# Block 0's first four shifts summed first, mean times power on GpSimd, and two weight slabs placed behind block 0's transposes

## The chip, the core and the metric

The kernel runs on one core of a Trainium2 chip. A core has five engines with an instruction queue each: TensorE (PE, matmuls), VectorE (DVE), ScalarE (ACT), GpSimd (POOL) and SyncE (SP, which here issues only transfers). Each works through its queue in order and waits at an instruction until the semaphores it needs have been raised. Transfers run on 16 DMA engines that all queues share. The metric is the device time of one execution in microseconds; lower is better.

## The reference

Four layers follow each other on one sequence of 2048 tokens with 1024 features: attention (A), feed-forward (B), and both again with the same weights. Each reads a normalised copy of the residual stream `x` and adds its result to it.

```
def _A_ref(x, wqkv, wo):
    H = 32; Dh = D // H;  W, dil = 8, 2
    q, k, v = split((x @ wqkv), heads)
    idx = pos[:, None] - dil * arange(W)[None, :]        # 8 keys: the own one and 7 earlier, 2 apart
    logits = einsum("bhsd,bhswd->bhsw", q, kg) * Dh**-0.5 # masked where idx < 0
    attn = softmax(logits)
    return einsum("bhsw,bhswd->bhsd", attn, vg) @ wo
def _B_ref(x, W_gate, W_up, W_down):
    return ((relu(x @ W_gate)) * (x @ W_up)) @ W_down     # F = 3584
x = x + _A_ref(_layernorm(x), A_wqkv, A_wo)
x = x + _B_ref(_layernorm(x), B_W_gate, B_W_up, B_W_down)
x = x + _A_ref(_layernorm(x), A_wqkv, A_wo)
x = x + _B_ref(_layernorm(x), B_W_gate, B_W_up, B_W_down)
```

The attention is a sliding window of 8 dilated positions, so its logits and its weighted sum are elementwise products and sums on VectorE; only the projections and the feed-forward are matmuls. All inputs are bf16.

## The kernel before

**Blocks and layers.** The tokens are cut into four blocks of 512 (four tiles of 128). For each layer L and block b there are steps: `plan_ln` (layer norm), `plan_proj` (q, k, v), `plan_attn` (logits, softmax, weighted sum), `plan_wo` (output projection and residual add), `plan_gu` (gate and up) and `plan_down`. L counts 0 (attention), 1 (feed-forward), 2 (attention), 3 (feed-forward).

**The order is written out by a planner.** Nothing is reordered later. Every step is put down with a planned time (`Plan.at`), and `Plan.run` (lines 116 to 120) sorts the steps by it and emits them; this fixes the order in every engine's queue. TensorE's planned time advances 0.216 us per matmul (`on_pe`). VectorE's steps come in two kinds. `plan.chain` is a long list, worked off in order, of the attention's products and sums. `plan.on_dve` steps (residual adds, gate multiplies, statistics) have a due time and go in between as soon as it is reached (`_place_dve`, lines 85 to 106). A load of a weight slab is placed when one of the five ring slots comes free, and not before the slab's `start` (`_place_slabs`, lines 108 to 114; `start` is -10.0 if nothing is given). The planner's times order the work; they are not the chip's.

**Weights.** Slabs are 1 MB (1024 rows by 512 columns) and go through the ring of five. `plan_gu` takes one gate and one up slab for four groups of 128 columns each.

**Layer norm.** `plan_ln` (lines 209 to 303) works on pairs of tiles. It gets sum and sum of squares from ScalarE (`stats`, lines 235 and 236), or statistics from VectorE (`bn`). `small_a` (239 to 258) computes mean and variance on VectorE and 1/sqrt on GpSimd as a power (line 257, or 247). `small_b` (260 to 263) multiplies -mean by it on VectorE. `norm` (265 to 270) applies both on ScalarE. `turn` (272 to 278) transposes a pair with a transfer issued by SyncE; the pair becomes half of `xnT`, the operand of the matmuls that follow.

**Block 0 of the first attention** has its logits computed in another layout (`first_logits`, lines 457 to 528). As each of the eight 128-row chunks of q and k leaves TensorE, VectorE multiplies it for all eight shifts (`mul`, line 488) and adds the product to two accumulators, shifts 0 to 3 (h=0) and 4 to 7 (h=1) (`add`, line 499). Each accumulator is then stored to DRAM (line 505), loaded again with heads on the partitions (line 510) and folded (`fold`, lines 524 and 525). Both accumulators end with the last chunk, so both stores, and both loads, follow each other closely. The softmax and the weighted sum (`pv_mul`, `pv_add`) come next, then the loads of the result (`load_o`, line 623) and the output projection `wo(0, 0)`. That is planned inside block 3's projection, behind its group ("q", 1, 1), by the table `wo_hook` (line 791).

**What follows wo(0, 0) on the engines.** TensorE goes on with the rest of block 3's q, with k and with v, and then starts `plan_gu(1, 0)`, which reads `xnT` of layer 1, block 0. On the other engines the residual adds (line 690), the norm and the two transposes of that block run meanwhile. On SyncE, between those transposes, stand loads of slabs for `plan_gu(1, 0)`, because two ring slots come free when block 3's k is done.

**Pools.** The tag "T" of the pool `tpose` has four buffers of 8 KB per partition, shared by `xnT`, the accumulators `lacc` and the attention outputs `oT`. The tags "q" and "k" of `hm_pool` have one buffer each.

Of the kernel before, what the change touches and what calls it, by code (L numbers as in the profile page):

```python
# [123 lines left out]
def kernel(  # L124
# [84 lines left out]
    def plan_ln(L, b, lag=0.5, on_vector=False, norm_at=0.0):  # L209
        hold = {}  # L210
        clock = [0.0]

        def begin():
            hold["xn"] = ln_pool.tile([P, TPB, D], BF16, tag="xn_all", name="xn_all")
            hold["T"] = tpose.tile([P, TPB, KC, P], BF16, tag="T", name=f"xnT_{L}_{b}")

        def bn(t):
            def f():
                if t == 0:
                    begin()  # L220
                if t % 2 == 0:
                    hold[("bn", t // 2)] = stat_pool.tile([P, 2, 2, 6], F32, tag="bst2", name="bst2")
                for h in range(2):
                    nc.vector.bn_stats(hold[("bn", t // 2)][:, t % 2, h, :], x_tiles[b * TPB + t][:, 512 * h:512 * h + 512])
            return f

        def stats(t):
            def f():
                if t == 0:
                    begin()  # L230
                if t % 2 == 0:
                    hold[("st", t // 2)] = stat_pool.tile([P, 2, 2], F32, tag="st", name=f"st_{L}_{b}")
                st, xt = hold[("st", t // 2)], x_tiles[b * TPB + t]
                junk = hold["xn"][:, t, :]
                nc.scalar.activation(junk, xt[:], ACT.Identity, accum_out=st[:, 0, t % 2:t % 2 + 1])
                nc.scalar.activation(junk, xt[:], ACT.Square, accum_out=st[:, 1, t % 2:t % 2 + 1])
            return f

        def small_a(p):
            rstd = stat_pool.tile([P, 2], F32, tag="rstd", name="rstd")  # L240
            vpe = stat_pool.tile([P, 2], F32, tag="vpe", name="vpe")
            if on_vector:
                mv = stat_pool.tile([P, 2, 2], F32, tag="mv2", name="mv2")
                for i in range(2):
# [5 lines left out]
            st = hold[("st", p)]  # L250
            mean = stat_pool.tile([P, 2], F32, tag="mean", name="mean")
            nc.vector.tensor_scalar(mean[:], st[:, 0, :], 1.0 / D, None, op0=ALU.mult)
            nvar = stat_pool.tile([P, 2], F32, tag="nvar", name="nvar")
            nc.vector.tensor_tensor(nvar[:], st[:, 0, :], mean[:], op=ALU.mult)
            nc.vector.tensor_tensor(nvar[:], nvar[:], st[:, 1, :], op=ALU.subtract)
            nc.vector.tensor_scalar(vpe[:], nvar[:], -1.0 / D, EPS, op0=ALU.mult, op1=ALU.add)
            nc.gpsimd.tensor_tensor(rstd[:], vpe[:], neg_half[:, 0:2], op=ALU.pow)
            hold[("mean", p)], hold[("rstd", p)] = mean[:], rstd

        def small_b(p):  # L260
            nb = stat_pool.tile([P, 2], F32, tag="nb", name="nb")
            nc.vector.scalar_tensor_tensor(nb[:], hold[("mean", p)], -1.0, hold[("rstd", p)][:], op0=ALU.mult, op1=ALU.mult)
            hold[("nb", p)] = nb

        def norm(t):
            def f():
                i, rstd, nb = t % 2, hold[("rstd", t // 2)], hold[("nb", t // 2)]
                nc.scalar.activation(hold["xn"][:, t, :], x_tiles[b * TPB + t][:], ACT.Identity,
                                     scale=rstd[:, i:i + 1], bias=nb[:, i:i + 1])
            return f  # L270

        def turn(t):
            def f():
                nc.sync.dma_start_transpose(hold["T"][:, t - 1:t + 1].rearrange("p t k n -> p (t k) n"),
                                            hold["xn"][:, t - 1:t + 1].rearrange("p t d -> p (t d)"))
                if t == TPB - 1:
                    xnT[(L, b)] = hold["T"]
            return f

        def row_done(t):  # L280
            def f(now):
                e = max(clock[0], now + 0.3)
                if on_vector:
                    plan.on_dve(e, 1.4, bn(t))
                    clock[0] = e + 1.4
                else:
                    plan.at(e, stats(t))
                    clock[0] = e + 2.6
                if t % 2 == 1:
                    plan.on_dve(clock[0], 0.7, lambda: small_a(t // 2), lambda n: after_a(n, t))  # L290
# [12 lines left out]
        return [row_done(t) for t in range(TPB)]  # L303
# [151 lines left out]


    def first_logits(st, tm):
        hold = {}

        def begin():  # L460
            hold["q"] = hm_pool.tile([P, KC, BLK], BF16, tag="q", name="q_fm")
# [3 lines left out]
        def evict(nm, c, acc, t):  # L465
            def f():
                if nm == "q":
                    nc.scalar.copy(hold["q"][:, c, :], acc()[:])
                    return
                kt = hold["k"]  # L470
                nc.scalar.copy(kt[:, c, HALO:HALO + BLK], acc()[:])
                nc.gpsimd.dma_start(_dram(k_d[1], c * ROW, [[D // P * ROW, P], [1, HALO]]),
                                    kt[:, c, BLK:BLK + HALO])
            if nm == "q" and c == 0:
                plan.at(t - 1.0, begin)
            plan.at(t, f)
# [8 lines left out]
        def mul(c):  # L485
            def f():
                pr = at_pool.tile([P, W, BLK], BF16, tag="pr", name=f"prod_{c}", bufs=2)
                nc.vector.tensor_tensor(pr[:], _ap(hold["q"], c * BLK, [[0, W], [1, BLK]]),
                                        _ap(hold["k"], c * ROW + HALO, [[-DIL, W], [1, BLK]]), op=ALU.mult)
                hold[("pr", c)] = pr  # L490
            return f

        def add(c, h):
            def f():
                if c == 1:
                    hold[("acc", h)] = tpose.tile([P, TPB, W // 2, P], F32, tag="T", name=f"lacc{h}")
                acc = hold[("acc", h)][:].rearrange("p q w t -> p w q t")
                first, more = (hold[("pr", i)][:, 4 * h:4 * h + 4].rearrange("p w (q t) -> p w q t", q=TPB) for i in (0, c))
                nc.vector.tensor_tensor(acc, first if c == 1 else acc, more, op=ALU.add)  # L499
            return f  # L500

        def turn(h):
# [15 lines left out]

        def fold(h):
# [181 lines left out]
    def plan_gu(L, b):  # L701
# [199 lines left out]
```

## Time and profile before

| | us |
|---|---|
| median of 3 runs | 1627.84 (1627.81 to 1628.78) |
| profiled execution | 1628.73 |
| its span, first to last instruction | 1627.0 |
| TensorE busy | 1610.5 (99%) |
| VectorE busy | 1059.3 (65%) |
| ScalarE busy | 441.7 (27%) |
| GpSimd busy | 104.2 (6%) |
| granted TensorE clock, mean | 0.998 |

Times in the views count from the span's start. A line of the order of time gives start, duration, engine, line of the kernel, operation, what it writes and reads, and in brackets how long the engine stood idle before it and what ended that. SPq and ACTq are issues of transfers; their durations are those of the issue. When a transfer has landed is told by a separate line, "DMA to landing". Waits name the engine and line that waited, what ended the wait, the sum, the count and the longest. The releaser is inferred from semaphores and can be the wrong one where an instruction waits for several.

### The profile page before, as it was taken

To read this page: it belongs to the slowest core of one execution; us is meant where nothing else is said; L and a number is where in the kernel's file an instruction comes from. 1 tells how busy PE (TensorE), PEld (TensorE's weight loads), DVE (VectorE), ACT (ScalarE), POOL (GpSimd) and SP (SyncE) were. 2 spreads that over 40 slices of the span, in tenths; PEclk is the share of its full clock that TensorE was granted. 3 is DMA by queue.
4 is the path that set the end of the run, shared out by engine and by line. 5 is a ranking of instruction groups with operands and counts; after the bars stand their busy time and mean duration, and the time that the engine had idled before them with its cause. 6 is when DMAs were issued, how large, how long until landed. Compare 5 with 4: busy or idle time off the path is not lost.

```text
span 1627.0 us, 19118 instructions
## 1 busy us (share of the span) xinstructions
PE 1610.5 (99%) x7577; PEld 745.2 (46%) x7626; DVE 1059.3 (65%) x1286; ACT 441.7 (27%) x701; POOL 104.2 (6%) x169
## 2 busy tenths in 40 slices
PE   9999899999999999999999999999999999999999
PEld 6444344444444444444444444444444444444444
DVE  6979889999999359870699716996989212211211
ACT  4642511304230341312413151133021301221110
POOL 2221000001000100011000110000000000000000
PEclk9999999999999999999999999999999999999999
DMA  8997767978956989568886699599846755665452
GB/s 249 219 245 162 201 153 203 217 198 203 240 161 193 258 192 225 172 210 222 199 214 188 197 235 215 159 281 243 217 152 196 196 168 162 174 177 160 156 163 69
DMA packets 445162, 319.01 MB, mean 196 GB/s; under 512 B 195696, under 2 KB 437776, under 8 KB 444816
## 3 DMA queue, kind: packets, MB, share of 16 engines
q1 hardware_dynamic: 415904, 285.59, 66.7%
q10 hardware_dynamic: 24368, 23.40, 4.9%
q0 software_dynamic: 4800, 8.80, 1.7%
q8 instruction: 59, 0.97, 0.3%
q14 instruction: 31, 0.25, 0.1%
HBM read 263.86 MB, written 38.15 MB: 186 GB/s over the span
## 4 chain that ended last, share of the span: by engine, by line
PE 89%; DVE 6%; DMA 2%; issue 1%; ACT 1%; POOL 0%; SPq 0%; ACTq 0%; DVEq 0%; POOLq 0%
PE acc_g L713 24%; PE acc_u L713 24%; PE dacc L759 24%; PE acc_wo L683 6%; PE acc_k L397 4%; PE acc_q L397 4%; PE acc_v L397 4%; DVE pvt L604 1%; DVE lacc L499 1%; DVE l L563 1%; DVE pvt L612 1%; DVE pr L553 1%; DMA v_d<-stage_v 0%; DMA lhm<-l_d 0%; DMA k_d<-stage_k 0%
## 5 line engine op out<-in xcount | busy, mean ns | idle before, releaser
L713 PEld LDWEIGHTS <-ring 128*128 128x128 bf16 x3584 | 350.9, 98 | 432.3 <-DMA v_d<-stage_v 7.7
L713 PE MATMUL acc_g<-xnT,ring 128*128 128x512 bf16 x1792 | 425.0, 380 | 7.2 <-DMA v_d<-stage_v 7.2
L713 PE MATMUL acc_u<-xnT,ring 128*128 128x512 bf16 x1792 | 423.9, 380 | 0.0
L759 PE MATMUL dacc<-ring,hT 128*128 128x512 bf16 (+1 forms) x1787 | 386.4, 376 | 1.7
L728 DVE TENSOR_TENSOR hT<-acc_u,r 128x512 bf16<-128x512 f32 x224 | 154.4, 689 | 329.1 <-PE acc_u L713 322.6
L720 ACT ACTIVATE r<-acc_g 128x512 bf16<-128x512 f32 x224 | 133.5, 596 | 713.1 <-PE acc_g L713 713.1
L759 PEld LDWEIGHTS <-hT 128*128 128x128 bf16 x1820 | 178.0, 98 | 209.1
L397 PEld LDWEIGHTS <-ring 128*128 128x128 bf16 x1152 | 115.5, 100 | 133.2 <-DMA ring<-in_A_wqkv_dram 0.3
L604 DVE TENSOR_TENSOR pvt<-a,vhm 128x4096 bf16<-128x4096 bf16 x64 | 146.2, 2284 | 0.2
L563 DVE TENSOR_TENSOR l<-l,pr 128x1024 f32<-128x1024 f32 x112 | 136.8, 1221 | 2.2
L553 DVE TENSOR_TENSOR pr<-qhm,khm 128x4096 bf16<-128x4096 bf16 x56 | 127.9, 2284 | 14.7 <-DMA khm<-k_d 14.7
L397 PE MATMUL acc_k<-xnT,ring 128*128 128x512 bf16 x512 | 113.2, 379 | 0.0
L683 PE MATMUL acc_wo<-ring,oT 128*128 128x512 bf16 x496 | 111.0, 379 | 0.8
L767 DVE TENSOR_TENSOR xb<-dacc,xb 128x512 bf16<-128x512 f32 (+1 forms) x49 | 32.6, 679 | 120.9 <-PE dacc L759 120.7
L397 PE MATMUL acc_v<-xnT,ring 128*128 128x512 bf16 x384 | 84.2, 379 | 0.0
L612 DVE TENSOR_TENSOR pvt<-pvt 128x2048 bf16<-128x2048 bf16 x64 | 78.1, 1221 | 1.3
L683 PEld LDWEIGHTS <-oT 128*128 128x128 bf16 x512 | 50.0, 98 | 60.5
L615 POOL DMA_DIRECT2D o_d<-ohm x64 | 35.2, 550 | 647.6 <-DVE ohm L614 634.5
L406 ACT CAST stage_q<-acc_q 128x512 bf16<-128x512 f32 x56 | 32.3, 582 | 153.6 <-PE acc_q L397 147.5
L563 DVE TENSOR_TENSOR l<-pr 128x1024 f32<-128x1024 bf16 x56 | 68.3, 1219 | 0.6
L570 DVE TENSOR_TENSOR l<-l 128x512 f32<-128x512 f32 x112 | 62.3, 556 | 2.9
L397 PEld LDWEIGHTS <-wqv 128*128 128x128 bf16 x480 | 44.8, 104 | 40.7 <-issue 1.4
(84 smaller groups left out, 807.8 us busy)
## 6 DMA issues: line engine op xcount, KB each, us to landing
ring<-in_B_W_gate_dram SPq DMA_DIRECT2D x56, 1024.0 KB, 7.3
ring<-in_B_W_up_dram SPq DMA_DIRECT2D x56, 1024.0 KB, 5.5
ring<-in_B_W_down_dram SPq DMA_DIRECT2D x48, 1024.0 KB, 6.0
ring<-in_A_wqkv_dram SPq DMA_DIRECT2D x26, 1024.0 KB, 5.4
ring<-in_A_wo_dram SPq DMA_DIRECT2D x16, 1024.0 KB, 7.1
vhm<-v_d SPq DMA_DIRECT2D x32, 284.0 KB, 7.1
v_d<-stage_v ACTq DMA_DIRECT2D x32, 256.0 KB, 7.0
o_d<-ohm POOLq DMA_DIRECT2D x64, 128.0 KB, 4.0
```

The costliest lines, as they stand in the source:

```text
L397: nc.tensor.matmul(acc[:, t0 * P:t1 * P], lhsT=lhsT, rhs=xnT[(L, b)][:, t0:t1, kc, :], start=(kc == 0), stop=(kc == KC - 1))
L553: nc.vector.tensor_tensor(pr[:], st["q"][:], _ap(st["k"], HALO - DIL * w, [[HALO + P, DH], [1, P]]), op=ALU.mult)
L563: nc.vector.tensor_tensor(l[:], pr[:, 0:8] if i == 0 else l[:], pr[:, 8 * i + 8:8 * i + 16], op=ALU.add)
L570: nc.vector.tensor_tensor(l[:, 0:n], l[:, 0:n], l[:, n:2 * n], op=ALU.add)
L604: nc.vector.tensor_tensor(tt[:], a_bc, v_sh, op=ALU.mult)
L612: nc.vector.tensor_tensor(tt[:, 0:4], tt[:, 0:4], tt[:, 4:8], op=ALU.add)
L615: nc.gpsimd.dma_start(_dram(o_d[b], g * DG * P, [[DH * P, P], [1, DG * P]]), o[:].rearrange("p d t -> p (d t)"))
L683: nc.tensor.matmul(acc[:], lhsT=st["oT"][:, c, t, :], rhs=ws[half]["t"][:, c, :], start=(c == 0), stop=(c == KC - 1))
L713: nc.tensor.matmul(acc[:], lhsT=w["t"][:, kc, (j % 4) * P:(j % 4 + 1) * P], rhs=xnT[(L, b)][:, :, kc, :], start=(kc == 0), stop=(kc == KC ...
L720: nc.scalar.activation(r[:], hold.pop(("g", j))[:], ACT.Relu)
L728: nc.vector.tensor_tensor(st["hT"][:, j, :], hold.pop(("u", j))[:], hold.pop(("r", j))[:], op=ALU.mult)
L759: nc.tensor.matmul(accs[(t, c0)][:], lhsT=st["hT"][:, j, t * P:(t + 1) * P], rhs=w["t"][:, jl, c0 - half * SLAB:c0 - half * SLAB + n], sta ...
```

## The change

There are five edits.

- In `first_logits`, chunks 0 to 3 stay as they are. Chunks 4 to 7 are multiplied in halves: first the four shifts of h=0 for all four chunks, each with its addition, then the four shifts of h=1. The h=0 accumulator's store and load are thus planned about 14 us ahead of those of h=1, and its fold stands directly behind the last addition. The h=0 load now goes to a buffer of the tag "T", the h=1 load to the tag "q". The planned time from an accumulator's end to its load's landing is 9.5 instead of 11.0.
- In `plan_ln`, -mean is kept in `neg` (VectorE), and GpSimd multiplies it by the power. `small_b` and its VectorE step are gone; `after` plans the normalise 1.8 behind `small_a`.
- In `plan_gu`, all slabs but the first pair of layer 1, block 0 may not be placed ahead of planned time 174.0. This touches the second pair only, since the others come later anyhow.
- `wo(0, 0)` is hooked behind the group ("q", 1, 0), eight matmuls earlier.
- The sign of the variance's parts is turned to suit `neg`; the number of instructions stays.

```
@@ plan_ln
         def small_a(p):
+            neg = stat_pool.tile([P, 2], F32, tag="neg", name="neg")
+            nb = stat_pool.tile([P, 2], F32, tag="nb", name="nb")
             if on_vector:
...
-                nc.gpsimd.tensor_tensor(rstd[:], vpe[:], neg_half[:, 0:2], op=ALU.pow)
-                hold[("mean", p)], hold[("rstd", p)] = mv[:, :, 0], rstd
-                return
+                nc.vector.tensor_scalar(neg[:], mv[:, :, 0], -1.0, None, op0=ALU.mult)
+            else:
+                st = hold[("st", p)]
+                nc.vector.tensor_scalar(neg[:], st[:, 0, :], -1.0 / D, None, op0=ALU.mult)
+                var = stat_pool.tile([P, 2], F32, tag="var", name="var")
+                nc.vector.tensor_tensor(var[:], st[:, 0, :], neg[:], op=ALU.mult)
+                nc.vector.tensor_tensor(var[:], var[:], st[:, 1, :], op=ALU.add)
+                nc.vector.tensor_scalar(vpe[:], var[:], 1.0 / D, EPS, op0=ALU.mult, op1=ALU.add)
             nc.gpsimd.tensor_tensor(rstd[:], vpe[:], neg_half[:, 0:2], op=ALU.pow)
-        def small_b(p):
-            nc.vector.scalar_tensor_tensor(nb[:], hold[("mean", p)], -1.0, hold[("rstd", p)][:], op0=ALU.mult, op1=ALU.mult)
+            nc.gpsimd.tensor_tensor(nb[:], neg[:], rstd[:], op=ALU.mult)
...
-        def after_a(now, t):
-            plan.on_dve(now + 1.3, 0.2, lambda: small_b(t // 2), lambda n: after_b(n, t))
-        def after_b(now, t):
-            e = max(clock[0], now + 0.2, norm_at)
+        def after(now, t):
+            e = max(clock[0], now + 1.8, norm_at)
@@ first_logits
             if nm == "k":
-                plan.chain.append((lambda: t + 0.7, 2.3, mul(c), None))
-                for h in range(2 if c else 0):
-                    plan.chain.append((lambda: 0.0, 2.3, add(c, h), turn(h) if c == KC - 1 else None))
+                ready[c] = t + 0.7
+                for h in range(2 if c == KC - 1 else 1):
+                    for c in range(KC // 2, KC) if h else (c,):
+                        whole = c < KC // 2
+                        plan.chain.append((lambda c=c: ready[c], 2.3 if whole else 1.2, mul(c, None if whole else h), None))
+                        for i in range(2 if whole else 1) if c else ():
+                            plan.chain.append((now, 2.3, add(c, i if whole else h), turn(h) if c == KC - 1 else None))
...
             def load():
-                hold[("l", h)] = hm_pool.tile([P, FG, W // 2, P], F32, tag="qk"[h], name=f"lhm{h}")
+                pool, tag = ((tpose, "T"), (hm_pool, "q"))[h]
+                hold[("l", h)] = pool.tile([P, FG, W // 2, P], F32, tag=tag, name=f"lhm{h}")
...
-                tm[("l_in", h)] = now + 11.0
+                tm[("l_in", h)] = now + 9.5
@@ plan_gu
-                sl = {"g": slab(wg_v[:, :, c0:c0 + SLAB], f"wg_{L}_{b}_{j // 4}"),
-                      "u": slab(wu_v[:, :, c0:c0 + SLAB], f"wu_{L}_{b}_{j // 4}")}
+                hold_back = 174.0 if (L, b) == (1, 0) and j else -10.0
+                sl = {"g": slab(wg_v[:, :, c0:c0 + SLAB], f"wg_{L}_{b}_{j // 4}", hold_back),
+                      "u": slab(wu_v[:, :, c0:c0 + SLAB], f"wu_{L}_{b}_{j // 4}", hold_back)}
@@
-    wo_hook = {("q", 1, 1): lambda: wo(0, 0)}
+    wo_hook = {("q", 1, 0): lambda: wo(0, 0)}
```

More of the change, by code (lines that the diff above doesn't have):

```diff
@@ L246, in small_a @@
                 nc.vector.tensor_scalar(vpe[:], mv[:, :, 1], EPS, None, op0=ALU.add)
-                nc.gpsimd.tensor_tensor(rstd[:], vpe[:], neg_half[:, 0:2], op=ALU.pow)
-                hold[("mean", p)], hold[("rstd", p)] = mv[:, :, 0], rstd
-                return
[L250 to L258, printed above, removed]
-        def small_b(p):
-            nb = stat_pool.tile([P, 2], F32, tag="nb", name="nb")
-            nc.vector.scalar_tensor_tensor(nb[:], hold[("mean", p)], -1.0, hold[("rstd", p)][:], op0=ALU.mult, op1=ALU.mult)
-            hold[("nb", p)] = nb
+                nc.vector.tensor_scalar(neg[:], mv[:, :, 0], -1.0, None, op0=ALU.mult)
[6 more added lines that the diff above has]
+                nc.vector.tensor_scalar(vpe[:], var[:], 1.0 / D, EPS, op0=ALU.mult, op1=ALU.add)
+            nc.gpsimd.tensor_tensor(rstd[:], vpe[:], neg_half[:, 0:2], op=ALU.pow)
+            nc.gpsimd.tensor_tensor(nb[:], neg[:], rstd[:], op=ALU.mult)
+            hold[("rstd", p)], hold[("nb", p)] = rstd, nb
         def norm(t):
@@ L289, in f @@
                 if t % 2 == 1:
-                    plan.on_dve(clock[0], 0.7, lambda: small_a(t // 2), lambda n: after_a(n, t))
+                    plan.on_dve(clock[0], 0.7, lambda: small_a(t // 2), lambda n: after(n, t))
             return f
-        def after_a(now, t):
-            plan.on_dve(now + 1.3, 0.2, lambda: small_b(t // 2), lambda n: after_b(n, t))
-        def after_b(now, t):
-            e = max(clock[0], now + 0.2, norm_at)
+        def after(now, t):
+            e = max(clock[0], now + 1.8, norm_at)
             plan.at(e, norm(t - 1))
@@ L457, in first_logits @@
     def first_logits(st, tm):
-        hold = {}
+        hold, ready = {}, {}
+        now = lambda: 0.0
         def begin():
@@ L483, in evict, with mul @@
                                        (lambda now: tm.__setitem__("logits", now)) if h else None))
-        def mul(c):
+        def mul(c, h):
             def f():
[L487 to L490, printed above, removed]
+                w, n = (0, W) if h is None else (W // 2 * h, W // 2)
+                pr = at_pool.tile([P, n, BLK], BF16, tag="pr", name=f"prod_{c}", bufs=2)
+                nc.vector.tensor_tensor(pr[:], _ap(hold["q"], c * BLK, [[0, n], [1, BLK]]),
+                                        _ap(hold["k"], c * ROW + HALO - DIL * w, [[-DIL, n], [1, BLK]]), op=ALU.mult)
+                for i in range(2) if h is None else (h,):
+                    hold[("pr", c, i)] = pr[:, W // 2 * i - w:W // 2 * (i + 1) - w].rearrange("p w (q t) -> p w q t", q=TPB)
             return f
@@ L497, in f @@
                 acc = hold[("acc", h)][:].rearrange("p q w t -> p w q t")
-                first, more = (hold[("pr", i)][:, 4 * h:4 * h + 4].rearrange("p w (q t) -> p w q t", q=TPB) for i in (0, c))
-                nc.vector.tensor_tensor(acc, first if c == 1 else acc, more, op=ALU.add)
+                nc.vector.tensor_tensor(acc, hold[("pr", 0, h)] if c == 1 else acc, hold[("pr", c, h)], op=ALU.add)
             return f
```

## The prediction

> **What bounds the kernel now.** I read the page first, then TensorE's waits, then the order of time around the one long wait, and last the engines ahead of it. The page:
>
> ```profile
> span 1627.0 us, 19118 instructions
> ...
> PE 1610.5 (99%) x7577; PEld 745.2 (46%) x7626; DVE 1059.3 (65%) x1286; ACT 441.7 (27%) x701; POOL 104.2 (6%) x169
> ```
>
> TensorE is busy for 1610.5 of 1627.0 us. The change takes no matmul away, so it can only win back idle or slowed matmul time. TensorE's own waits, all of them:
>
> ```profile
> PE acc_g L713 <- DMA v_d<-stage_v: 7.2, 1, 7.2
> PE warm L317 <- POOL neg_half L183: 1.4, 1, 1.4
> PE acc_v L397 <- DVE xnT L359: 0.9, 1, 0.9
> PE acc_v L397 <- ACT xnT L359: 0.5, 2, 0.2
> PE tp L356 <- DVE xn_all L351: 0.4, 1, 0.4
> ```
>
> One wait matters: 7.2 us ahead of the first gate matmul. The name of its releaser misleads, as the order of time (cut to SyncE, one ScalarE store and TensorE) shows:
>
> ```profile
> 176.58 1.97 SPq L274 DMA_TRANSPOSE xnT<-xn_all  x1
> ...
> 178.65 1.48 SPq L199 DMA_DIRECT2D ring<-in_B_W_gate_dram  x1
> ...
> 181.30 0.37 ACTq L414 DMA_DIRECT2D k_d<-stage_k  x1
> ...
> 183.60 0.37 SPq L199 DMA_DIRECT2D ring<-in_B_W_up_dram  x1
> ...
> 188.62 4.04 SPq L274 DMA_TRANSPOSE xnT<-xn_all  x1
> ...
> 198.75 3.57 PE L713 MATMUL acc_g<-xnT,ring 128*128 128x512 bf16 x8 [7.24 <-DMA v_d<-stage_v]
> ```
>
> The transpose at 188.62 writes the second half of the activations that acc_g reads. Asked for alone, line 274 has this landing in the stretch from 188 to 192, and this over the whole run:
>
> ```profile
> DMA to landing us min/median/max: 10.0/10.0/10.0
> ```
> ```profile
> DMA to landing us min/median/max: 4.4/7.1/11.9
> ```
>
> So it lands at 198.66, and acc_g starts at 198.75. Its data were there at 180.80 (the last normalise, 179.56 plus 1.24). SyncE handles its queue in order: it stood until 183.60 before the up slab, then until the landing of the k store of 181.30:
>
> ```profile
> SPq L274 <- DMA k_d<-stage_k: 4.6, 1, 4.6
> ```
>
> The transpose does not read that store. In the program SyncE's and ScalarE's transfers take eight semaphores in turn, and each waits for the landing of the one eight places ahead; the two slabs are two of those places. The stall's full price is in the windows (columns: length, PE, PEld, DVE, ACT, POOL busy, granted clock, DMA share, GB/s):
>
> ```profile
> 184.40:191.50 7.10, 7.10 (x33) 3.03 (x31) 6.89 (x8) 2.24 (x4) 0.00 (x0) 1.00 1.22 307
> 191.50:198.75 7.25, 0.01 (x2) 0.03 (x1) 5.52 (x6) 0.58 (x1) 0.00 (x0) 0.84 1.09 215
> 198.75:204.40 5.65, 5.65 (x17) 2.12 (x18) 0.00 (x0) 0.60 (x1) 0.00 (x0) 0.61 0.23 79
> ```
>
> After the idle stretch the granted clock is 0.61 for 5.65 us. The last v matmuls start at 184.44, and 32 matmuls take 6.91, so acc_g could start at 191.35: 7.40 us lost. Its first 16 matmuls end with the next acc_g at 204.39, so they take 5.64; the following 16 take 3.45 (204.39 to 207.84). That is 2.19 more. **The whole stall costs 9.59 us**, the most that can be won here.
>
> **The change part by part.**
>
> *The gated slabs.* Two loads of 1 MB (second gate and up slab of layer 1, block 0) move behind the second transpose on SyncE. In the planner's times (the numbers its steps are sorted by, not those of the chip) they stand at 167.2 now and at 174.0 after. The second transpose stands at 168.7 now; following its row of planned steps through the new code gives 165.9. So the order does turn. SyncE is then free once the first transpose is issued (176.0 plus 1.97), and two places fewer separate the second from its semaphore's last user. That user becomes, by the places in the program of before, a q store issued near 172 to 175, landed within 4.5 us (the page's median for these stores); at worst it is the first k store, see the first rival. What waits behind the gate: the slabs are issued near 184 instead of 178.65 and 183.60. With their measured 8.1 and 9.4 us they land by 194. They are needed for the fifth pair of matmul groups, 4 x 3.45 us after 191.35, at 205.2. Cost nothing; the 11 us between cover it.
>
> *wo(0,0) one group earlier.* Eight matmuls (1.73 us) move from before it to behind it; TensorE's sum is unchanged. It starts at 153.35 - 1.73 = 151.62. Its first operand landed at 147.10 + 4.2 = 151.3 before, so even without a faster chain it fits, by 0.3 us. The residual adds, ScalarE's sums and the normalise start 1.5 to 1.7 us earlier. But one q eviction (0.56) and its store's issue (0.44) now also stand between ScalarE's last sums and the normalise. Counted through: sums end at 171.3 (172.78 - 1.5); two evictions and one issue to 172.8; normalise 1.13; eviction and issue to 174.85; normalise to 176.0; eviction, normalise, eviction, issue, normalise (0.5, 1.15, 0.5, 0.44, 1.15) to 179.8. Data at 179.8 instead of 180.80: 1.0 us won.
>
> *Mean and power on GpSimd.* Per pair one VectorE instruction of 0.16 us goes (the sums' variant; the other swaps it for another of 0.16), and with it VectorE's wait for GpSimd. A GpSimd multiply of 128x2 appears in no row. Bounds: 0.21 (its smallest memset) to 2.67 (the power below, which ran beside VectorE's bf16 multiply). I take 0.71, the usual power on the same shape. In exchange ScalarE's normalise waits for GpSimd. On the path above: power 173.5 to 175.0 (1.52 there), multiply to 175.7, needed at 176.5: hidden by the k eviction. With 2.67 it is 177.7, and the data come at 181.0. A gain there is excluded, since ScalarE is the later one. Two rows decide the rest:
>
> ```profile
> 58.28 0.16 DVE L262 SCALAR_TENSOR_TENSOR nb<-mean,rstd 128x2 f32<-128x2 f32 x1 [1.80 <-POOL rstd L257]
> ```
> ```profile
> 61.46 2.67 POOL L257 TENSOR_TENSOR rstd<-vpe,neg_half 128x2 f32<-128x2 f32 x1 [3.22 <-DVE vpe L256]
> ```
>
> Block 0's sums stand behind these waits: 1.80 + 0.59 + two instructions, 2.7 us won on VectorE.
>
> The Trainium skill (GPSIMD Engine Reference, 8. Key points) speaks against this move: it has VectorE about twice as fast in elementwise work and GpSimd contending with it for SBUF. The row of 2.67 agrees on the contention; by twice VectorE's 0.16 the multiply would be an estimated 0.3, and neither changes the sum.
>
> *First four shifts ahead.* Four multiplies of 2.28 become eight of 1.22 (the row of a 128x2048 bf16 operation): 4 x 0.24 with their gaps, 1.0 us more. The sums of h=0 end near 67, so VectorE also waits some 0.5 for ScalarE's statistics. The last sum ends at 82.2 - 2.7 + 1.0 + 0.6 = 81.1. The first store goes behind the block-2 transpose on SyncE, at 71 to 72.5; with 4.9 to 6.9 us it lands at 76 to 79.4, and its load (8.0) at 84 to 87.5. SyncE stands between the two, with one v load and the second store queued behind; the v load moves from 73.4 to about 79, needed at 105. VectorE now meets fold(0) at 81.1, ahead of block 3's statistics, and stands there 3 to 6 us; then 1.9 for the fold and 6.2 for the statistics bring it to 95.6 at most. The second store (81.2 + 6.9) and load (7.8) land at 96.0, against 97.00. So 1.0 us won; bounds 3 won (4.9 for the store) and 3 lost (the three 1 MB transfers all beside each other). No end reaches TensorE by itself except through wo(0,0).
>
> **Sum.** Second transpose issued at 179.8, landing 7.1 later (median; the first had 7.1 as well) at 186.9, needed at 191.35. With the longest landing, 11.9, it is 191.7. The wait goes, the slow clock with it: 1628.73 - 9.59 = 1619.1 against the profiled execution, which is 0.9 above the median 1627.84; against the median **1618.3 us**. Next late is block 1's attention output, below.
>
> **Rivals.**
> 1. *The transpose still comes late.* If its semaphore's last user is the first k store (issued near 179, 6.0 to landing) it goes out at 185, and with 7.1 to 10.0 lands at 192 to 195: a stall of 0.7 to 3.7, and up to 2.2 of slow clock. 1619 to 1624, say 1621. For it: it happened before in just this way. Against: two places fewer, and no slab beside it (the DMA share was 1.22). The Trainium skill (TensorE: Matmul & The Clock Gate, Part 1: The HAM clock gate) has the clock halved only after about 3.4 us of idling; by it the shorter stalls here would cost themselves alone. The windows above show only a 7.25 us idle followed by 0.61, which agrees.
> 2. *Block 0's chain comes late at wo(0,0)*, by up to 3 us less the 0.3 in hand: 1618.3 + 1.7 to 2.7, some 1620.5. For it: the load that VectorE meets early, and the small margin. Against: 2.7 us of waits gone.
> 3. *The gain is given back at wo(0,1).* Its four operand pieces landed at 291.9, 295.1, 298.1, 304.1 and are used from 297.63 on, 3.45 apart: the last has 3.9 us in hand. If they did not move, 5.7 of 9.6 would be lost: 1624.0. Against: SyncE issues them between slabs that TensorE releases, and VectorE idled 7.5 us for acc_u in the stall, so both come forward.
> 4. *Slower.* The h=0 load now lives in the buffers of the transposed activations. If it gets the one that block 1's v matmuls read until 94.7, SyncE stands there with store and load of h=1 behind: 94.7 + 0.4 + 6.9 + 7.8 = 109.8, 12.8 later than 97.00. Then wo(0,0) stands 12.5, plus 2.2, less 9.6: 1633. It decides from a delay of about 7.7. Against: block 3's transpose went out at 94.34, before those matmuls' end, so it took a buffer that block 0's sums had left; the load finds the same one.
> 5. *No change*: another wait of the same length, e.g. slabs that stay ahead.
>
> **How the numbers follow.** Forecast 0.60 (own range 1617.3 to 1619.3: the scatter of 1.0 us shown by the runs); rival 1 0.15; rival 2 0.06; rival 3 0.07; rival 4 0.08; rival 5 0.04. Measurement tells 0.2%, 3.3 us. Faster takes the first four less 0.01 of their ends: 0.87; same 0.05; slower 0.08. The range 1617.3 to 1624.0 keeps the forecast and rivals 1 to 3, some 0.85.
>
> **What would show it.** Right: no TensorE wait near 190, granted clock 1.00 there, both transposes issued before the second gate slab, the second landing before 191. wo(0,0) starts near 151.6 with no gap; no VectorE wait for GpSimd; first l_d store near 72. Wrong: a wait at acc_g with the transpose landing last, a gap at an acc_wo, or SyncE standing until about 94 ahead of the h=0 load.

## The result and the profile after

The changed kernel takes 1619.44 us (median of 6 runs, 1619.23 to 1619.50) beside 1627.51 for the kernel before (6 runs, 1624.87 to 1628.78): a ratio of 0.9953, 95% interval 0.9941 to 0.9966, or 5.5 to 9.6 us. Forecast: 1618.3, range 1617.3 to 1624.0, faster. The profiled execution took 1619.48 us with a span of 1617.7; against 1628.73 before, that is 9.25 us.

The page of the changed kernel, span and busy times:

```profile
span 1617.7 us, 19190 instructions
...
PE 1610.6 (100%) x7626; PEld 745.1 (46%) x7626; DVE 1057.0 (65%) x1264; ACT 440.7 (27%) x701; POOL 124.9 (8%) x199
```

TensorE's busy time is about what it was (1610.5; the page of before lacks 49 of the 7626 matmul records, so the two compare only roughly), and the span has shrunk onto it. All of TensorE's waits in the changed kernel:

```profile
PE warm L310 <- POOL neg_half L183: 1.4, 1, 1.4
PE acc_v L390 <- DMA wqv<-in_A_wqkv_dram: 1.0, 1, 1.0
PE tp L349 <- DVE xn_all L344: 0.6, 1, 0.6
PE acc_v L390 <- ACT xnT L352: 0.5, 2, 0.2
PE acc_wo L684 <- DMA oT<-o_d: 0.2, 1, 0.2
```

The 7.2 us at acc_g is gone. New are 1.0 us at the start, for a weight load that the diff does not touch (0.9 stood there before, for another operand), and 0.2 us at wo(0,0). SyncE's order of time around the second transpose:

```profile
183.62 2.12 SPq L270 DMA_TRANSPOSE xnT<-xn_all  x1
185.83 1.37 SPq L199 DMA_DIRECT2D ring<-in_B_W_gate_dram  x1
189.34 0.37 SPq L199 DMA_DIRECT2D ring<-in_B_W_up_dram  x1
```

and its landing, line 270 asked for alone at that time:

```profile
DMA to landing us min/median/max: 6.6/6.6/6.6
```

The transpose now stands ahead of both slabs. It goes out at 183.62, 0.03 after its data (the last normalise, 182.35 plus 1.24), and lands at 190.20. TensorE, in order of time:

```profile
187.77 4.05 PE L390 MATMUL acc_v<-xnT,ring 128*128 128x512 bf16 x18
191.65 1.89 PE L714 MATMUL acc_g<-xnT,ring 128*128 128x512 bf16 x8
193.38 1.89 PE L714 MATMUL acc_u<-xnT,ring 128*128 128x512 bf16 x8
```

acc_g starts at 191.65 without a gap, with 1.45 us in hand, and its eight matmuls take 1.89 us where they took 3.57. The windows over this stretch (columns as in the prediction) have the clock at full speed:

```profile
184.40:191.50 7.10, 7.10 (x35) 3.21 (x34) 6.89 (x8) 3.22 (x6) 0.00 (x0) 1.00 1.00 209
191.65:197.30 5.65, 5.65 (x28) 2.58 (x27) 5.48 (x7) 1.94 (x4) 0.00 (x0) 1.00 1.09 382
```

From acc_g to wo(0,1) it is now 288.35 - 191.65 = 96.70 us, against 297.63 - 198.75 = 98.88: the 2.18 of slow clock that the prediction had as 2.19.

The rest did not go as forecast. The multiply on GpSimd is short, but the second transpose's data come 2.8 us later than before (183.59 against 180.80), not 1.0 earlier. And the second load of block 0's logits is later. VectorE's fold(1) in the changed kernel, after a wait for that load, stands at 98.63, where it stood at 97.12:

```profile
98.63 1.23 DVE L525 TENSOR_TENSOR lhm<-lhm 128x1024 f32<-128x1024 f32 x1 [4.46 <-DMA lhm<-l_d]
```

### The profile page after: what moved, and what is told of

Its sections match the earlier page's. It is cut to its first block, busy times and chain, and to the rows that moved or that the text cites. A ratio compares the mean times of both kernels' runs of the same rounds, so it can differ in the third digit from the quotient of the medians.

```text
span 1617.7 us, 19190 instructions
## 1 busy us (share of the span) xinstructions
PE 1610.6 (100%) x7626; PEld 745.1 (46%) x7626; DVE 1057.0 (65%) x1264; ACT 440.7 (27%) x701; POOL 124.9 (8%) x199
## 4 chain that ended last, share of the span: by engine, by line
PE 92%; DVE 3%; DMA 3%; ACT 1%; issue 1%; POOL 0%; SPq 0%; ACTq 0%; DVEq 0%; POOLq 0%
PE acc_g L714 24%; PE acc_u L714 24%; PE dacc L761 24%; PE acc_wo L684 7%; PE acc_k L390 5%; PE acc_v L390 5%; PE acc_q L390 5%; DVE pvt L605 1%; DMA l_d<-lacc 1%; DVE pvt L613 1%; DMA q_d<-stage_q 0%; DMA x<-in_A_x_dram 0%; DMA k_d<-stage_k 0%; DVE pvt L614 0%; DMA lhm<-l_d 0%
## 5 line engine op out<-in xcount | busy, mean ns | idle before, releaser
L257 POOL TENSOR_TENSOR rstd<-vpe,neg_half 128x2 f32<-128x2 f32 x30 | 32.2, 1074 | 541.8 <-DVE vpe L256 533.2
L264 ACT ACTIVATE xn_all<-xb,nb,rstd 128x1024 bf16<-128x1024 bf16 x48 | 57.7, 1235 | 30.4 <-POOL nb L258 27.9
```

## The experiments

**Theory A** after the result: the place of the two slabs carries the whole gain, and the other three edits give nothing or cost. **Rival R**: the earlier projection, the sums and the multiply on GpSimd do part of it. About the slabs themselves there are two readings. **S**: they pushed the transpose back in the turn of the eight semaphores, so that it waited for a store. **Q**: their 2 MB of traffic slowed the transpose and what it waits for. "In hand" below is the time from the second transpose's landing to TensorE's need for it. The kernel before is measured beside each set, and its median is 1629.16 on the chip of the first four runs, 1628.39 on that of the next four and 1625.98 on that of the last four, so times of different sets are compared through it with care.

### The slabs alone

```
-  sl = {"g": slab(wg_v[...], f"wg_{L}_{b}_{j // 4}"),
-        "u": slab(wu_v[...], f"wu_{L}_{b}_{j // 4}")}
+  hold_back = 174.0 if (L, b) == (1, 0) and j else -10.0
+  sl = {"g": slab(wg_v[...], f"wg_{L}_{b}_{j // 4}", hold_back),
+        "u": slab(wu_v[...], f"wu_{L}_{b}_{j // 4}", hold_back)}
```

> The kernel before, with only the two slabs held back. Theory A (the order of the two slabs alone carries the whole gain): the second transpose of layer 1, block 0 goes out as soon as its data are there, at 180.85 (the last normalise of before ended at 180.80), because its semaphore's turn is now two places earlier and falls on a transfer that landed before 175. It lands at 186 to 190, the wait of 7.2 us at the gate matmuls and the 2.19 of slow clock behind it go, and the time is that of the changed kernel, 1619.4, within 0.5 us. Rival R (the earlier output projection, the sums and the multiply on GpSimd bring the transpose forward and carry part of the gain): a wait of 1 us or more stays at the first gate matmul, and the time is 1621 to 1625.

Measured: 1618.59 us (1618.45 to 1619.21), ratio 0.9935 (0.9923 to 0.9948). SyncE's order of time in this kernel:

```profile
181.09 2.16 SPq L274 DMA_TRANSPOSE xnT<-xn_all  x1
183.34 1.33 SPq L199 DMA_DIRECT2D ring<-in_B_W_gate_dram  x1
```

The transpose lands at 187.62 (6.5 after its issue), 3.34 in hand, and no wait is left at acc_g. Theory A has the mechanism; the time is even 0.3 below its band, which raised the question whether the other edits cost. The runs of one chip, further down, answer it.

### All but the slabs

```
-  hold_back = 174.0 if (L, b) == (1, 0) and j else -10.0
-  ... slab(..., hold_back)
+  ... slab(...)
```

> The changed kernel with the two slabs back in front of the second transpose. Theory A: the transpose's semaphore turn falls on a k store again, which is issued near 184 with the changed order of ScalarE's work and lands near 189, so the transpose goes out at 189 to 191 and lands at 196 to 201. TensorE needs it at 191.65: a wait of 5 to 9 us, and 2 us of slow clock; 1627 to 1630, no better than the kernel before. Rival R: the earlier start of the projection takes the wait below 4 us, and the time is 1623 or less.

Measured: 1626.95 us (1625.51 to 1628.16), ratio 0.9986 (0.9977 to 0.9995). TensorE's wait and the order of time on the two queues of this kernel:

```profile
PE acc_g L714 <- DMA v_d<-stage_v: 5.9, 1, 5.9
```
```profile
183.68 0.37 ACTq L407 DMA_DIRECT2D k_d<-stage_k  x1
...
186.31 0.37 SPq L199 DMA_DIRECT2D ring<-in_B_W_up_dram  x1
187.27 5.17 SPq L270 DMA_TRANSPOSE xnT<-xn_all  x1
```

The k store of 183.68 landed at 187.20 and the transpose followed at 187.27, with 10.2 us to its landing at 197.50. The stall is back. Theory A expected no gain at all; there is one of 2.2 us, under the 0.2% that the prediction called telling. So alone the three edits are worth 0.8 to 3.7 us by the interval; in the traced execution the stall is still there and 1.3 us shorter. R's "below 4 us" is not reached.

### The turn of the semaphores without the slabs' traffic

The slabs held back as above, and in their old place four loads of 4 KB into a tile that nobody reads:

```
+  tiny = const.tile([P, 4, 16], BF16, name="tiny")
+  for i in range(4):
+      plan.at(167.2, lambda i=i: nc.sync.dma_start(tiny[:, i], x_dram[0:P, 16 * i:16 * i + 16]))
```

> The kernel before with the two slabs held back, and in their old place on SyncE four loads of 4 KB each that nobody reads. They give the second transpose its old place in the turn of the eight semaphores without the slabs' 2 MB. Theory S (the turn of the semaphores is what kept the transpose): it waits for a k store again, goes out at 183.5 to 187 and lands at 190 to 195; TensorE needs it at 191.35, so a wait of 0 to 4 us, and 1619.3 to 1625 in all. Theory Q (the slabs' own traffic, or SyncE's stand before them, kept it): it goes out at 180.85, without a wait for any store, lands before 190, and the time is 1619.3.

Measured: 1619.13 us (1619.09 to 1619.34), ratio 0.9944 (0.9929 to 0.9959). The two queues of this kernel in order of time, and SyncE's wait:

```profile
181.71 0.37 ACTq L415 DMA_DIRECT2D k_d<-stage_k  x1
...
186.19 1.94 SPq L275 DMA_TRANSPOSE xnT<-xn_all  x1
```
```profile
SPq L275 <- DMA k_d<-stage_k: 2.7, 1, 2.7
```

S is shown for the issue: four transfers of 4 KB hold the transpose until the k store of 181.71 has landed (186.12), though it does not read it; without them it went out at 181.09. But it then lands after 4.8 us, at 191.03, and TensorE loses 0.27:

```profile
DMA to landing us min/median/max: 4.8/4.8/4.8
```

The turn without the slabs' traffic therefore costs next to nothing here. The store that it waits for takes 4.4 us, against 7.25 before, and the transpose 4.84 against 10.04. Those differences, 2.84 and 5.20, are together 8.0 us, about the whole stall of 7.24; the k store was issued 0.41 later here.

### The turn shortened, one slab's traffic kept

Only the up slab is held back; the gate slab stays ahead of the transpose:

```
   sl = {"g": slab(wg_v[...], f"wg_{L}_{b}_{j // 4}"),
-        "u": slab(wu_v[...], f"wu_{L}_{b}_{j // 4}")}
+        "u": slab(wu_v[...], f"wu_{L}_{b}_{j // 4}", hold_back)}
```

> The kernel before with only the up slab held back; the gate slab stays ahead of the second transpose. Theory S: one place fewer in the turn, so the transpose's semaphore falls on the first k store, issued near 179 and landed by 185; and SyncE no longer stands before the up slab. The transpose goes out at 180.9 to 185 and lands at 188 to 194 beside the gate slab: a wait of 0 to 2.6 us, 1619.3 to 1622. Theory Q (the slabs' traffic keeps the transpose): it lands 10 us after its issue, as it did before beside both slabs: at 191 or later, a wait of 0 to 4 us; a landing of less than 8 us speaks against Q.

Measured: 1621.89 us (1620.47 to 1623.43), ratio 0.9961 (0.9947 to 0.9974). In its order of time the gate slab comes first, and the transpose when the first k store (178.06) has landed, at 184.00:

```profile
179.17 1.44 SPq L199 DMA_DIRECT2D ring<-in_B_W_gate_dram  x1
...
184.07 5.06 SPq L274 DMA_TRANSPOSE xnT<-xn_all  x1
```
```profile
DMA to landing us min/median/max: 10.1/10.1/10.1
```

S gave the issue (180.9 to 185), Q the 10 us to the landing at 194.14. The wait of 3.15 us is longer than S allowed. It is that of the slowest of the four executions (1623.43); two others, at 1620.47 and 1620.94, have a mean granted clock of 1.000 against 0.999, so the clock hardly fell there and the wait was probably shorter. Neither reading holds alone: the turn makes the transpose wait for a store, and beside the slabs' traffic the store and the transpose take longer. In the three kernels with a slab issued ahead and still in flight, the landing of this transpose took 10.0, 10.2 and 10.1 us; in those without, 4.8 to 9.3. That is no rule for other transposes: in the kernel before, the one at 319.00 has a slab 0.5 us ahead of it and lands after 7.5 us, and the one at 94.34 has none in flight and takes 9.1. Moving both slabs takes away the turn and the traffic ahead.

One kernel is missing: both slabs ahead, but no store to wait for. An estimate from rows of before is that there would be no stall: data at 180.80 and 10.0 us to the landing make 190.8, ahead of the 191.35 at which acc_g could start. By it the turn and the traffic were both needed.

The windows of this kernel around the wait:

```profile
191.12:194.27 3.15, 0.00 (x1) 0.03 (x1) 3.05 (x4) 0.82 (x2) 0.00 (x0) 0.90 1.12 282
194.27:196.77 2.50, 2.50 (x6) 0.86 (x7) 2.43 (x4) 0.00 (x0) 0.00 (x0) 0.50 1.09 369
```

After 3.15 us without work the granted clock is 0.50 for 2.5 us. From acc_g to wo(0,1) it is 98.05 us, 1.35 more than without a stall.

### The projection three groups later

```
-    wo_hook = {("q", 1, 0): lambda: wo(0, 0)}
+    wo_hook = {("q", 1, 3): lambda: wo(0, 0)}
```

> The changed kernel with the output projection three groups later (about 5.2 us). The residual adds, the normalise and both transposes of layer 1, block 0 move with it, while TensorE reaches the gate matmuls at the same 191.65. The second transpose's data come near 188.8 and it lands near 195.4: a wait of 3 to 5 us in place of none. If an idle of that length lowers the granted clock as the 7.25 us did, 2 us of slow matmuls come on top: 1624 to 1626.5; if it does not, 1622 to 1624.5.

Measured: 1626.50 us (1625.26 to 1627.27), ratio 0.9988 (0.9979 to 0.9997). The transpose goes out at 189.16 and lands at 196.46:

```profile
PE acc_g L714 <- DMA xnT<-xn_all: 5.7, 1, 5.7
```
```profile
196.59:198.60 2.01, 2.01 (x5) 0.70 (x6) 1.98 (x2) 0.00 (x0) 0.00 (x0) 0.50 1.07 313
198.60:200.60 2.00, 2.00 (x6) 0.73 (x5) 0.78 (x1) 0.40 (x1) 0.00 (x0) 0.50 1.10 374
```

(the wait, and two windows after it). The wait is 0.65 above the band, and acc_g to wo(0,1) takes 99.53, so the slow clock costs 2.83 more. A late transpose costs as much when late data make it so as when slabs do: nearly all of the gain is lost with the slabs still behind it.

### All but the first four shifts, all but GpSimd, all but the hook

The first takes `first_logits` from the kernel before, the second `small_a`, `small_b` and what calls them:

```
-   nc.gpsimd.tensor_tensor(nb[:], neg[:], rstd[:], op=ALU.mult)
+   nc.vector.scalar_tensor_tensor(nb[:], hold[("mean", p)], -1.0, hold[("rstd", p)][:], op0=ALU.mult, op1=ALU.mult)
```

and the third only the hook:

```
-    wo_hook = {("q", 1, 0): lambda: wo(0, 0)}
+    wo_hook = {("q", 1, 1): lambda: wo(0, 0)}
```

> The changed kernel with block 0's sums in the order of before (both halves end together, one after the other). In the changed kernel the second load of the logits landed at 98.61, 1.5 us later than before, and the first output projection waited 0.2 us for its operand. Theory A: this part gives nothing, so the time is 1619.4 within 0.5 us; the second load lands at 95 to 97.5, and the wait of 0.2 us at the output projection goes. Rival R: VectorE's earlier or later work moves the second transpose's data by more than its 1.45 us in hand, a wait comes back at the gate matmuls, and the time is 1621 or more.

> The changed kernel with the product of mean and reciprocal deviation on VectorE again. Theory A: this part gives nothing either; 1619.4 within 0.5 us, the second transpose's data at 180 to 184 against 183.59, no wait at the gate matmuls. Rival R: with VectorE's waits for GpSimd back (1.8 us in one row, 0.3 to 0.6 in others) block 0's sums end 2 to 3 us later, the second logits load lands 2 to 3 us later, and the output projection waits up to 3 us for its operand: 1620.5 to 1623.

> The changed kernel with the output projection of block 0 one group later, where it was. The projection starts at 153.65 instead of 151.93 and no longer waits 0.2 us for its operand; everything behind it up to the second transpose comes up to 1.7 us later. In the changed kernel that transpose's data were there at 183.59 and it landed 1.45 us before it was needed. Theory A: the move of the projection gives nothing but this slack; the transpose's data come at 181 to 185.5, it lands at 188 to 192.5, a wait of 0 to 1 us; 1619.2 to 1620.5. Rival R: the move is part of the gain; a wait of 1.5 us or more at the gate matmuls, 1621 to 1623.

Measured: without the first four shifts 1619.38 us (1618.69 to 1623.74), ratio 0.9944 (0.9932 to 0.9957); without GpSimd 1620.94 (1620.21 to 1625.78), 0.9955 (0.9942 to 0.9967); without the hook 1619.82 (1619.19 to 1620.09), 0.9947 (0.9934 to 0.9959).

The first agrees with A in the time and not in the reason. The second load landed at 98.58, not at 95 to 97.5, and wo(0,0) waited 0.42. So the later load is not the work of the first four shifts alone. In the second, R's wait at wo(0,0) shows:

```profile
PE acc_wo L691 <- DMA oT<-o_d: 1.0, 1, 1.0
```

though the load is only 0.4 later than in the changed kernel (99.01 against 98.61), not 2 to 3; the time is R's, 2.35 us over the slabs alone on the same chip. This points to the multiply on GpSimd earning something beside the other two edits, by less waiting at wo(0,0) (0.17 in the changed kernel, 0.99 here); the changed kernel was not run on this chip, so it is not shown. In the third, the transpose landed at 191.26, and TensorE waited 0.27, as A had it. In all three the transpose lands 0.1 late to 0.5 early, so each is near the edge of a stall. The upper runs of the first two (1623.74, 1625.78) may be such stalls: their mean granted clock is 0.999 and 0.998, that of the other runs 1.000. No trace of them is kept.

### The hook alone, GpSimd alone, and the whole beside the slabs alone, on one chip

Each on top of the slabs held back: the hook at ("q", 1, 0); or the changed kernel's `small_a` and `after`; then the slabs alone and the changed kernel again.

```
-    wo_hook = {("q", 1, 1): lambda: wo(0, 0)}
+    wo_hook = {("q", 1, 0): lambda: wo(0, 0)}
```
```
-        def after_b(now, t):
-            e = max(clock[0], now + 0.2, norm_at)
+        def after(now, t):
+            e = max(clock[0], now + 1.8, norm_at)
```

> The kernel before with the slabs held back and the output projection of block 0 one group earlier, and nothing else. With the slabs alone the projection started at 152.98 without a wait, and the second transpose landed at 187.62, 3.3 us before it was needed. Theory A (the early projection costs, whatever its company): it waits 0 to 1 us for its operand; q evictions come between the statistics and the normalise, so the second transpose's data come 1.5 to 2.5 us later than with the slabs alone, and it lands at 190 to 192; 1619 to 1621, that is 0.4 to 2 us over the slabs alone. Rival R (only the chain of the first four shifts made it costly): no wait at the projection, 1618.6.

> The kernel before with the slabs held back and the multiply on GpSimd, and nothing else. Theory A: the multiply is worth nothing where no wait is left on TensorE; within 0.5 us of the slabs alone (1618.6). The first transpose goes out 1 to 2 us earlier than with the slabs alone (176.84) and the second's data come later than 181.09, since the first pair's normalise comes ahead of the later rows' statistics: 182 to 184, landing 188 to 191. Rival R: the later data bring a wait of 0.3 us or more at the gate matmuls, 1619 to 1620.

> The kernel before with only the two slabs held back, once more, beside the changed kernel on one chip. If the other three edits cost, as 1618.59 against 1619.44 on two chips has it, it is 0.4 to 1.2 us faster than the changed kernel here too; if that was the chips' difference, the two agree within 0.3 us.

> The changed kernel, once more, beside the kernel with only the slabs held back: 1619.0 to 1619.8, 0.4 to 1.2 us slower than that one if the other three edits cost; within 0.3 us of it if they do not. Its second transpose lands 0.5 to 2 us before it is needed, against 3.3 us with the slabs alone.

Measured on one chip, the kernel before at 1625.98 us (9 runs, 1624.48 to 1627.01):

| kernel | median us (5 runs) | ratio, 95% | second transpose issued, landed | needed |
|---|---|---|---|---|
| slabs alone | 1618.85 (1618.70 to 1619.06) | 0.9956 (0.9944, 0.9969) | 180.52, 187.94 | 191.24 |
| slabs and hook | 1618.91 (1618.68 to 1619.86) | 0.9958 (0.9945, 0.9972) | 179.57, 187.02 | 190.86 |
| slabs and GpSimd | 1619.47 (1618.57 to 1620.09) | 0.9959 (0.9947, 0.9972) | 182.02, 191.37 | 191.07 |
| changed kernel | 1619.03 (1618.63 to 1619.76) | 0.9958 (0.9946, 0.9971) | 183.19, 191.00 | 191.87 |

The slabs alone and the changed kernel are 0.18 us apart. The 0.85 between the first two measurements of them is thus not shown to be the edits' cost; chips and scatter cover it. What is shown is that the other edits give nothing that these runs, which scatter by up to 1.5 us, can tell once the stall is gone.

For the hook A fell: the data come 0.95 us earlier than with the slabs alone, and wo(0,0) starts at 151.15 without a wait. For GpSimd R held, with a wait of 0.43 at acc_g. ScalarE's order says why the data are later. With the slabs alone:

```profile
171.31 1.06 ACT L236 ACTIVATE xn_all<-x 128x1024 bf16<-128x1024 bf16 x1
...
173.86 2.38 ACT L268 ACTIVATE xn_all<-x,nb,rstd 128x1024 bf16<-128x1024 bf16 x2 [0.44 <-DVE mean L252]
...
177.64 1.24 ACT L268 ACTIVATE xn_all<-x,nb,rstd 128x1024 bf16<-128x1024 bf16 x1 [0.45 <-ACT stage_k L406]
...
179.25 1.24 ACT L268 ACTIVATE xn_all<-x,nb,rstd 128x1024 bf16<-128x1024 bf16 x1
```

With the slabs and GpSimd:

```profile
170.06 1.23 ACT L264 ACTIVATE xn_all<-x,nb,rstd 128x1024 bf16<-128x1024 bf16 x1
...
171.66 1.25 ACT L264 ACTIVATE xn_all<-x,nb,rstd 128x1024 bf16<-128x1024 bf16 x1
...
175.06 1.06 ACT L236 ACTIVATE xn_all<-x 128x1024 bf16<-128x1024 bf16 x1
...
178.59 1.24 ACT L264 ACTIVATE xn_all<-x,nb,rstd 128x1024 bf16<-128x1024 bf16 x1 [0.34 <-POOL nb L258]
...
180.75 1.24 ACT L264 ACTIVATE xn_all<-x,nb,rstd 128x1024 bf16<-128x1024 bf16 x1 [0.45 <-ACT stage_k L399]
```

Line 236 is the last statistic. With one step fewer between `small_a` and the normalise, the planner puts the first pair's normalises ahead of the last row's statistics instead of behind them; this order stands in all kernels with the edit and in none without it. The first transpose goes out 3.3 us earlier (172.93 against 176.26), which nobody needs. The last statistic comes 3.75 later (175.06 against 171.31), and the transpose that TensorE waits for 1.5 later (182.02 against 180.52).

## Why the prediction was right, and where it was not

**The stall and its price: right.** 9.59 us were forecast for the profiled execution (1619.1) and 9.25 measured (1619.48). Of the 0.34 between, 0.30 is the start of acc_g (191.65 for 191.35). It arises at wo(0,0): the group ahead of it starts at 149.87 (149.90 before), and wo(0,0) at 151.93 instead of the 151.62 forecast, the wait for its operand that rival 2 had in view.

**The median: 1.1 us too low.** The step that failed was taking the 0.9 by which the profiled run of before stood over its median off the forecast as well. The kernel before scatters over 3.9 us here; without the stall the changed kernel's six runs lie within 0.3 us, and within 1.1 in the later set. So most of the scatter went with the stall, and the 0.9 was probably a part of the 9.59 already. That this excess lay in the stall is argued: only one execution of before was traced.

**The gated slabs: right in what they do, incomplete in why.** The prediction gave the gain to the queue and the turn of the semaphores, and took 2.9 us off the landing (7.1 for 10.0). The four tiny loads show that the turn alone does not make the stall: with the turn in place and no slab ahead it is 0.27 us. With one slab ahead and a shorter turn it is 3.15. The traffic is thus needed for it; that the turn is needed too rests on the estimate further up. The slabs cost nothing in their new place: they land at 195.03 and 199.33, up to 5 later than forecast, and TensorE shows no wait for them.

**The second transpose's data: wrong, 183.59 for 179.8.** The count through ScalarE's queue holds for the hook alone (179.57, and 0.95 us won against 1.0 forecast). Two steps failed. The step on GpSimd asked only how long the multiply takes and which eviction hides it, and kept the order of ScalarE's work. The planner's order changed, and the data came 1.5 us later with that edit alone. The step on the sums let them reach TensorE through wo(0,0) alone. But with hook and sums and no multiply on GpSimd, where ScalarE keeps its order, the data come at 182.88, 3.3 later than with the hook alone. There wo(0,0) starts 1.22 later (152.37 against 151.15), and the block's first statistic, which waits for a residual add on VectorE, 2.62 later (162.42 against 159.80); why VectorE is that late stays open. The delays do not add up: with all three edits it is 3.6 (183.19 against 179.57 on one chip). Of the 4.45 us in hand that the forecast implied (191.35 - 186.9), 3.8 went; a landing 0.5 shorter and a need 0.3 later gave some back, and 1.45 were left. A late transpose was nearer than rival 1's 0.15 says, though not by rival 1's road: it went out 0.03 after its data, without a wait for a store.

**The multiply: 0.71 taken, 0.20 measured.** Line 258 of the changed kernel, its spread over 30:

```profile
L258 POOL TENSOR_TENSOR nb<-neg,rstd x30: 188/196/2288, 22.7 to 1426.6; 128x2 f32<-128x2 f32 x30
```

The smallest memset (0.21) was the nearer row, not the power, and even a little long as the lower bound. The longest, 2.29, lies inside the bounds.

**The first four shifts: wrong in sign.** The last sum ended at 80.9 (81.1 forecast) and the first store went out at 71.36 (71 to 72.5). But the second store went out at 82.31 (81.2 forecast) and landed at 93.06, 10.75 after its issue, where 6.9 had been taken from before: the step carried a landing over from a stretch with other transfers beside it. Its load took 5.5 instead of 7.8 and gave some back. The second load came 1.6 us late instead of 1.0 early, inside the bound of 3 lost, and showed as rival 2's wait, 0.2 us. Which edits make it late stays open: it landed at 98.2 to 99.0 in every kernel that has the hook and at least one more of the three edits, with the slabs held back or not, at 97.95 with the projection three groups later, and at 96.3 to 97.5 in the others.

**The rivals.** Rival 3 (given back at wo(0,1)) did not happen: 96.70 us after acc_g, without a wait. Rival 4 (the buffer that block 1 still reads) neither: the load went out at 79.43, 0.07 after its store had landed. Rival 1 allowed up to 2.2 of slow clock; the sentence in it by which shorter stalls would cost themselves alone does not hold at 3.15 us, see below.

## What to carry to other kernels

When a transfer is late, ask separately what it waited for before it was issued, and what was in flight ahead of it: here a turn of shared semaphores and two large loads made one stall together, the turn without the loads made almost none, and a shorter turn with one load a shorter one. An edit that shortens a chain can reorder the work around it, so follow the order that the planner will write out, not only the durations; of two pairs it may speed up the one that nobody waits for. Once an engine is busy from end to end, further edits that "help" only move the margin of the next wait: measure that margin, because the time does not show it.

## What was not expected of the hardware

**A wait of 3.15 us already halves the clock, and the clock stays low for 3.4 or 6.8 us.** The prediction had seen slow matmuls behind the wait of 7.24 us only. The first column is the wait at acc_g, the second the time from its start to the drop of the granted clock to 0.50, the third how long the clock stayed there (from windows of 0.1 us), and the last what the time from acc_g to wo(0,1) has over the 96.70 without a stall.

| wait at acc_g, us | drop after, us | clock at 0.50 for, us | slow clock costs, us |
|---|---|---|---|
| 0.27 (two kernels) | none | none | 0.0 |
| 3.15 | 2.51 | 3.42 | 1.35 |
| 5.65 | 4.60 | 6.83 | 2.83 |
| 5.94 | 2.75 | 6.83 | 1.77 |
| 7.24 | 4.88 | 6.82 | 2.18 |

The windows of the low clock behind the waits of 3.15 and 7.24 us:

```profile
193.63:197.05 3.42, 2.78 (x7) 1.04 (x8) 3.32 (x5) 0.00 (x0) 0.00 (x0) 0.50 1.09 364
```
```profile
196.39:203.21 6.82, 4.46 (x11) 1.66 (x12) 0.77 (x1) 0.60 (x1) 0.00 (x0) 0.50 0.55 158
```

The price is half of the low stretch that falls behind the wait: 2.78 us of matmuls in the first (half is 1.39, against 1.35 measured) and 4.46 in the second (2.23 against 2.18). So it depends on when the clock dropped and not on the length of the wait alone: 5.65 us cost more than 7.24.

The Trainium skill (TensorE: Matmul & The Clock Gate, Part 1: The HAM clock gate) has the clock drop after an idle window of about 3.4 us that runs freely. Its half speed agrees with the 0.50 here, and the low stretches of 3.42 and 6.82 to 6.83 us are once and twice its figure; a window that runs freely would fit the differing drops and prices. That a wait of 3.15 us was enough is a little below its figure, and the measurement decides.

**The same transpose lands after 4.8 to 10.2 us.** The three landings of 10 have a slab ahead of it still in flight; the longest without one took 9.3. What spreads the rest from 4.8 to 9.3, with the slabs behind, was not tried.
